# Making the third 512-row block of four rounds use seven products in its second layer, and planning with shorter tables

## The chip, the cores and the metric

The kernel runs on one core of a Trainium2 chip. The metric is the device time of one execution in microseconds (us); the median of three runs stands for a kernel. A profile of one further execution, taken by the hardware profiler, gives the start and length of every instruction on each engine: PE (TensorE matmuls; PEld its weight loads), DVE (VectorE), ACT (ScalarE), POOL (GpSimd) and SP (SyncE, which here only issues DMAs).

## What is computed

The input is x of shape (8, 2496, 256): eight batches of 2496 rows. The first half is a two-dimensional Fourier transform of every batch, of which the real part is kept:

```python
X = np.fft.fft(x, axis=1)
X = np.fft.fft(X, axis=2)
x = X.real.reshape(19968, 256)
```

The second half sends each of the 19968 rows to one of 8 experts, a network of two layers with 1024 hidden values, and weighs the result:

```python
logits = x @ w_gate
e = np.argmax(logits, axis=1)
h = np.maximum(x[rows of e] @ w1[e], 0.0)
y[rows of e] = h @ w2[e]
out = gate_w[:, None] * y
```

## The kernel before

**Two streams of work in one program.** The *mixing* of a batch (functions `first`, `second` and `route`, L325 to L460) computes the transform, the logits and the place of each row, and `send` (L462) scatters rows, 128 at a time, with an indirect DMA of POOL into a buffer `Xs` sorted by expert. The *experts* (`experts`, L728) take blocks of rows of one expert out of `Xs`, run both layers and scatter the result to the output, again with indirect DMAs of POOL (`put_row`, L235). Which block belongs to which expert is found on the chip by `plan` (L478), a chain of small DVE instructions on one partition. Its tables have `MOST` entries, 21, the largest number of blocks of any plan.

**Rounds.** `rounds()` (L130) fixes how many blocks are formed of each batch: small ones for batches 0 and 1, three blocks of 512 rows for batch 2, five blocks of 512 rows for each of the batches 3 to 6, and five of 512, seven of 256 and up to 21 of 128 for batch 7. While the blocks of batch b are worked on, the mixing of batch b+1 and the first 12 steps (`AHEAD`, L186) of that of batch b+2 are woven in. The main loop (L985 to L1018) lets `experts` run from `yield` to `yield` and, by a count of the work done, puts a step of mixing behind some of them; steps are given out over the first 60% (`SHARE`) of a round's second layers. In the first-layer part of a 512-row block only sends are put in. The order of all instructions on every engine is therefore written by this program; each engine works through its own list in that order.

**Blocks by seven products.** The first layer of every 512-row block of batches 3 to 7 is made with seven products of half size in place of eight (`seven`, L613; the choice is `halved`, L191). Its sums are made by DVE out of PSUM and written to `hT` (L634 to L653). The second layer of some blocks is made by seven products as well (`lower`, L659; the choice is `quartered`, L196): in batches 3 to 6 the blocks with index 3 and 4, in batch 7 all of its 512- and 256-row blocks. Otherwise the second layer is the plain one (L874 to L885): for each 128 rows eight matmuls into a PSUM tile `py`, one scaling by ACT (L881), one indirect DMA.

What `lower` needs beyond the plain form:

- sums of weights (`Below`, L593 to L606): four additions of 128x512 on POOL for a 512-row block. If the block before it is plain, they are issued between that block's four `py` parts (`soon`, L875); otherwise in the block's own first layer (`below.step()`, L814);
- sums of hidden values: four DVE instructions at L809 in the first layer, two at L860 (`s2`) and two at L864 (`s4`) in the second;
- five PSUM banks shared with the first layer (`pse`, one buffer each of a to e), and after the products six DVE additions on halves of `y` (L682, L700, L706, L712) and ACT scalings (L678, L687).

While a block's second layer runs, the next block's rows are turned (`turn`, L576): per 256 rows a DVE transpose (L582) and an ACT change of sign (L585), then four DVE additions (L570 to L573). The mixing steps put their own DVE instructions (the fold of `xq`, L295 to L306; L408 and L410 for the rows) and ACT copies (`t<-pr` L372, `zz` L379, `zs` L405) into the same lists, and share one pool of three PSUM buffers (`pm_`) for `pr`, `p`, `s` and `rk`.

Of the kernel before, what the change touches and what calls it, by code (L numbers as in the profile page):

```python
# [15 lines left out]
ALU = mybir.AluOpType  # L16
ACTF = mybir.ActivationFunctionType
AX_X = mybir.AxisListType.X
PSUM = bass.MemoryType.PSUM

B, S, D = 8, 2496, 256
# [14 lines left out]
E, F = 8, 1024  # L36
# [14 lines left out]
def bc(ap, axis, n):  # L51
    shape = list(ap.shape)
    shape.insert(axis, n)
    return ap[tuple([slice(None)] * axis + [None])].to_broadcast(shape)
# [75 lines left out]
def rounds():  # L130

    want = [((256, 2), (128, 4)), ((256, 4),)] + [((512, B),)] * (B - 2)
    plan, used = [], 0

    def full(done, size):
        return max(0, -(-(done - used - E * (size - 1)) // size))

    for b in range(B):  # L140
        done = (b + 1) * S
        now = []
        for size, most in want[b]:
            k = min(full(done, size), most)
            if k:
                now.append((size, k, False))
            used += size * k
        if b == B - 1:
            k = full(done, BLK)
            used += BLK * k  # L150
            now.append((BLK, k, False))
            now.append((REST, (NT - used + E * (REST - 1)) // REST, True))
        plan.append(now)
    return plan
# [33 lines left out]
MOST = max(k for now in rounds() for _, k, _ in now)  # L188


def halved(b, size):  # L191

    return size == 512 and b > 2 or size == 256 and b == B - 1


def quartered(b, size, at):  # L196

    return halved(b, size) and (b == B - 1 or at >= 3)


def block_consts():
# [14 lines left out]
def kernel(ctx: ExitStack, tc, x, w_gate, w1, w2, out):  # L216
    nc = tc.nc
    vec, act, pool = nc.vector, nc.scalar, nc.gpsimd
# [50 lines left out]
    con, k = {}, 0  # L269
# [205 lines left out]
    bk = {n: bt[:, lo:hi] for n, (lo, hi) in where.items()}  # L475
    gone = bk["cap"]

    def plan(b, size, k, last):  # L478

        nonlocal gone  # L480

        def one(name, *dims, dt=F32):
            return cp.tile([1, *dims], dt, tag="p_" + name, name="p_" + name, bufs=2 if name == "gone" else 1)

        nb, ni = one("nb", E), one("ni", E, dt=I32)
        ce, ex, rb, n = one("ce", E), one("ex", E), one("rb", E), one("n", E)
        lo = one("lo", E, E)
        vec.tensor_tensor(nb[:], base[0:1], gone[:], op=ALU.subtract)
        vec.tensor_scalar(ni[:], nb[:], size - 1.0 if last else 0.0, None, op0=ALU.add)
        vec.tensor_scalar(ni[:], ni[:], size.bit_length() - 1, None, op0=ALU.logical_shift_right)  # L490
        vec.tensor_copy(nb[:], ni[:])
        vec.tensor_tensor(lo[:], bk["low"].rearrange("p (a b) -> p a b", a=E), bc(nb[:], 1, E), op=ALU.mult)
        vec.reduce_sum(ce[:], lo[:], axis=AX_X)
        vec.tensor_tensor(ex[:], ce[:], nb[:], op=ALU.subtract)
        yield
        vec.scalar_tensor_tensor(rb[:], ex[:], -float(size), gone[:], op0=ALU.mult, op1=ALU.add)
        ge, ei = one("ge", MOST, E), one("ei", MOST)
        val, eq, rw = one("val", MOST, E + 1), one("eq", MOST, E + 1), one("rw", MOST)
        vec.tensor_tensor(ge[:], bc(bk["i"], 2, E), bc(ce[:], 1, MOST), op=ALU.is_ge)
        vec.reduce_sum(ei[:], ge[:], axis=AX_X)  # L500
        yield
        vec.tensor_tensor(eq[:], bc(ei[:], 2, E + 1), bc(bk["e9"], 1, MOST), op=ALU.is_equal)
        vec.memset(val[:, :, E:E + 1], float(E * CAP))
        vec.scalar_tensor_tensor(val[:, :, 0:E], bc(bk["i"], 2, E), float(size), bc(rb[:], 1, MOST),
                                 op0=ALU.mult, op1=ALU.add)
        yield
        vec.tensor_tensor(val[:], val[:], eq[:], op=ALU.mult)
        vec.reduce_sum(rw[:], val[:], axis=AX_X)
        tab = cp.tile([1, 2, MOST], I32, tag="p_tab", name="p_tab", bufs=4)
        vec.tensor_copy(tab[:, 0], rw[:])  # L510
        vec.tensor_scalar(tab[:, 1], ei[:], E - 1.0, None, op0=ALU.min)
        if last:
            cnt = cp.tile([1, 1], I32, name="cnt")
            vec.tensor_copy(cnt[:], ce[:, E - 1:E])
            tabs["cnt"] = cnt
        if not last:

            vec.tensor_scalar(n[:], ex[:], -1.0, float(k), op0=ALU.mult, op1=ALU.add)
            vec.scalar_tensor_tensor(n[:], n[:], 0.0, nb[:], op0=ALU.max, op1=ALU.min)
            nxt = one("gone", E)  # L520
            vec.scalar_tensor_tensor(nxt[:], n[:], float(size), gone[:], op0=ALU.mult, op1=ALU.add)
            gone = nxt
        yield
        tabs[b, size, last] = tab
# [203 lines left out]
    def experts(todo):  # L728
# [35 lines left out]
        for k, (b, size, last, at) in enumerate(todo):  # L764
# [24 lines left out]
            def step():  # L789
                if chores:  # L790
                    chores.popleft()()
                elif more:
                    more.step()

            both = quartered(b, size, at)
            below = None
            if both:
# [36 lines left out]
            if follow:  # L834
                while follow[:3] not in tabs:
                    yield 0, False
                fetch_some(k + 1, 2)
                while follow[0] not in whole:
                    yield 0, follow[0] < LATE
                fetch_some(k + 1, 2)  # L840
                turned = turn(*follow[:2], xbs[0][0])
                if halved(*follow[:2]):
                    left = more or Left(got[0][0])
                if not both and size == follow[1] == BIG and quartered(*follow[:2], follow[3]):
                    soon = Below(got[0][1], pool)
# [61 lines left out]
    def close(b):  # L907

        for size, k, last in rounds()[b]:
            yield from plan(b, size, k, last)  # L910
# [158 lines left out]
```

## Time and profile before

| | |
|---|---|
| median of three runs | 1270.7 us (1270.32 to 1275.03) |
| the profiled execution | 1270.37 us, of which the span from first to last instruction is 1268.5 us |
| busy in the span | PE 1212.5 us, PEld 1083.6, DVE 773.6, POOL 445.7, ACT 421.5 |
| granted TensorE clock | 0.980 of full speed on the mean, 1.00 from 300 us to 1240 us |
| second layer of the third block (index 2) | batch 3: 419.80 to 441.82 us, batch 4: 564.83 to 586.85, batch 5: 709.86 to 728.78, batch 6: 848.39 to 862.21 |

How to read the views: the page's first part gives busy time, share of the span and number of instructions for each engine. In a group or a timeline row, the line is that of kernel.py, then come engine, operation, output<-inputs and shapes; L221 is the helper that records every matmul, so matmuls are told apart by their output tile. In the timeline, the first number is the start in us from the beginning of the span, the second how long the merged row lasted; `x16` is the number of instructions merged, and a bracket says how long the engine had been idle before and what ended that. One fp32 matmul appears as two rows' worth of records, so that `x16` are eight matmuls.

### The profile page before, as it was taken

The page shows a single profiled execution, that of the slowest core. Times are in us where ns is not written, and L with a number is a line of the kernel's source. Part 1 is how long each engine was busy: PE and PEld are TensorE (multiplying, and loading weights), DVE is VectorE, ACT ScalarE, POOL GpSimd, SP SyncE. Part 2 cuts the span into 40 slices and gives each one's busy share as a digit, 9 for nine tenths or more (in the row PEclk, how much of TensorE's full clock was granted, in tenths as well). Part 3 has the DMA queues.
Part 4 walks back from the last instruction along what each step waited for, and adds up shares of the span by engine and source line. Part 5 has one row for each costly group of instructions (what it writes and reads, how often), then busy time and mean ns, then how long its engine had stood idle before and what let it go on. Part 6 is the DMA issues. An engine that isn't in the chain of part 4 may idle for free.

```text
span 1268.5 us, 22212 instructions
## 1 busy us (share of the span) xinstructions
PE 1212.5 (96%) x7289; PEld 1083.6 (85%) x7289; DVE 773.6 (61%) x1884; ACT 421.5 (33%) x1087; POOL 445.7 (35%) x527
## 2 busy tenths in 40 slices
PE   5759999999999999999999999999999999999996
PEld 4548987876788899888998999889999999999995
DVE  4546334443465788576866588686788884444662
ACT  1423332332243433434243433432332322222222
POOL 0145427145116522472226612561462331111112
PEclk9869999999999999999999999999999999999997
DMA  8769898765348454573336435443444348777786
GB/s 239 246 194 334 306 311 305 193 223 176 124 151 254 139 148 154 165 249 114 101 127 207 136 117 171 133 153 96 146 130 159 104 157 288 278 284 270 270 292 231
DMA packets 163216, 249.79 MB, mean 197 GB/s; under 512 B 118601, under 2 KB 130227, under 8 KB 143516
## 3 DMA queue, kind: packets, MB, share of 16 engines
q1 hardware_dynamic: 146327, 203.28, 49.9%
q0 software_dynamic: 15888, 42.14, 9.2%
q10 hardware_dynamic: 885, 2.94, 0.7%
q8 instruction: 59, 0.97, 0.3%
q14 instruction: 57, 0.47, 0.1%
HBM read 194.91 MB, written 54.83 MB: 197 GB/s over the span
## 4 chain that ended last, share of the span: by engine, by line
PE 71%; issue 16%; DMA 4%; POOL 4%; DVE 3%; ACT 0%; POOLq 0%; SPq 0%; DVEq 0%; ACTq 0%
PE py L221 19%; PE a L221 10%; PE c L221 10%; PE d L221 7%; PE ph L221 6%; PE p L221 6%; PE b L221 5%; PE e L221 3%; PE s L221 3%; POOL out_dram L236 3%; DMA xq<-in_x_dram 1%; POOL Xs L236 1%; DMA t<-Td 1%; DMA w<-c_w 1%; DMA Xs<-rows,pi 0%
## 5 line engine op out<-in xcount | busy, mean ns | idle before, releaser
L236 POOL DMA_INDIRECT out_dram<-y,ro x163 | 161.0, 988 | 633.8 <-ACT y L678 297.9
L221 PE MATMUL py<-w_sb,hT 128*128 128x256 f32 x1504 | 340.3, 380 | 0.0
L221 PEld LDWEIGHTS py<-w_sb,hT 128*128 128x128 f32 x1504 | 282.0, 191 | 36.1 <-issue 1.0
L236 POOL DMA_INDIRECT Xs<-rows,pi x160 | 163.7, 1023 | 113.7 <-DVE rows L410 55.0
L221 PE MATMUL ph<-xT,w_sb 128*128 128x128 f32 (+2 forms) x992 | 173.0, 331 | 9.8 <-DVE ro L782 8.7
L221 PEld LDWEIGHTS ph<-xT,w_sb 128*128 128x128 f32 x992 | 137.7, 194 | 34.2 <-issue 16.5
L221 PE MATMUL a<-xT,w_sb 128*128 128x256 f32 (+1 forms) x512 | 118.1, 358 | 0.3 <-DVE xT L582 0.2
L827 DVE TENSOR_SCALAR hT<-ph 128x512 f32<-128x512 f32 x43 | 29.7, 690 | 127.7 <-PE ph L221 68.9
L585 ACT ACTIVATE xT<-xT 128x256 f32<-128x256 f32 (+1 forms) x94 | 36.5, 388 | 185.8 <-DVE xT L582 135.7
L221 PEld LDWEIGHTS a<-xT,w_sb 128*128 128x128 f32 x512 | 88.6, 191 | 10.6 <-DVE xT L582 1.3
L881 ACT ACTIVATE y<-py,xb 128x256 f32<-128x256 f32 x97 | 45.8, 473 | 154.4 <-PE py L221 152.6
L634 DVE TENSOR_TENSOR hT<-hT,b 128x512 f32<-128x512 f32 x57 | 39.2, 688 | 80.6 <-PE b L221 53.9
L408 DVE COPY lg<-p 128x16 f32<-128x16 f32 x80 | 13.8, 172 | 113.8 <-ACT zs L405 113.7
L644 ACT ACTIVATE hT<-a 128x512 f32<-128x512 f32 x57 | 34.0, 597 | 140.2 <-PE a L221 140.2
L221 PE MATMUL s<-xq,w 104*112 104x256 f32 (+2 forms) x208 | 61.5, 420 | 11.6 <-DVE xq L297 8.9
L582 DVE STREAM_TRANSPOSE xT<-xb 128x512 f32<-128x512 f32 (+1 forms) x94 | 58.7, 627 | 12.7 <-DMA xb<-Xs 12.7
L469 POOL CAST pi<-due 128x1 int32<-128x1 f32 x140 | 42.2, 301 | 68.8 <-ACT due L468 68.7
L221 PE MATMUL a<-w_sb,hT 128*128 128x128 f32 x528 | 66.0, 276 | 0.0
L221 PE MATMUL p<-table,zz 128*128 128x145 f32 (+1 forms) x320 | 58.3, 308 | 8.0 <-DVE rows L410 6.6
L221 PE MATMUL d<-w_sb,hT 128*128 128x128 f32 x528 | 65.5, 275 | 0.0
L221 PEld LDWEIGHTS a<-w_sb,hT 128*128 128x128 f32 x528 | 63.2, 192 | 0.7
L221 PEld LDWEIGHTS d<-w_sb,hT 128*128 128x128 f32 x528 | 62.2, 192 | 0.0
(144 smaller groups left out, 2086.0 us busy)
## 6 DMA issues: line engine op xcount, KB each, us to landing
w_sb<-in_moe_w_dram SPq DMA_DIRECT2D x132, 1024.0 KB, 7.0
xq<-in_x_dram SPq DMA_DIRECT2D x24, 896.0 KB, 8.6
xb<-Xs SPq DMA_DIRECT2D x112, 128.0 KB, 3.3
Td<-t SPq DMA_DIRECT2D x18, 448.0 KB, 3.3
t<-Td SPq DMA_DIRECT2D x8, 768.0 KB, 9.5
t<-Td SPq DMA_DIRECT2D x8, 640.0 KB, 9.2
xb<-Xs SPq DMA_DIRECT2D x52, 64.0 KB, 5.9
xb<-Xs SPq DMA_DIRECT2D x100, 32.0 KB, 5.4
```

What stands on the lines that cost most here:

```text
L221: nc.tensor.matmul(o, lhsT=lhsT, rhs=rhs, start=start, stop=stop, **kw)
L236: return unordered(pool.indirect_dma_start(out=dst, out_offset=bass.IndirectOffsetOnAxis(ap=idx, axis=0), in_=rows, in_offset=None, bounds ...
L408: vec.tensor_copy(lg[:, k:k + 2], p3[:, NY:NY + 2 * E].rearrange("p (m e) -> p m e", m=2))
L469: pool.tensor_copy(idx, due[:])
L582: vec.transpose(free(xT[:], 256 * h, [32, n // 32], [BIG, 2], [1, 32]), free(xb, 512 * h, [64, n // 32], [1, 2], [2, 32]))
L585: act.activation(odd, odd, ACTF.Copy, scale=-1.0)
L634: vec.tensor_tensor(h12, h11, b[:], op=add)
L644: act.activation(h11, a[:], ACTF.Relu)
L827: vec.tensor_scalar(o, ph[:], 0.0, None, op0=ALU.max)
L881: act.activation(y[:, i % 2], py[:], ACTF.Copy, scale=meta[:, i, 1:2])
```

## The change

Index 2 is added to the blocks whose second layer is made by seven products, which concerns one block in each of the batches 3 to 6. In `plan`, the tables get as many entries as the plan has blocks (k) in place of 21.

```diff
 def quartered(b, size, at):
 
-    return halved(b, size) and (b == B - 1 or at >= 3)
+    return halved(b, size) and (b == B - 1 or at >= 2)
...
         vec.scalar_tensor_tensor(rb[:], ex[:], -float(size), gone[:], op0=ALU.mult, op1=ALU.add)
-        ge, ei = one("ge", MOST, E), one("ei", MOST)
-        val, eq, rw = one("val", MOST, E + 1), one("eq", MOST, E + 1), one("rw", MOST)
-        vec.tensor_tensor(ge[:], bc(bk["i"], 2, E), bc(ce[:], 1, MOST), op=ALU.is_ge)
-        vec.reduce_sum(ei[:], ge[:], axis=AX_X)
+        ge, val, eq = (one(name, MOST, E + 1)[:, 0:k] for name in ("ge", "val", "eq"))
+        ei, rw = (one(name, MOST)[:, 0:k] for name in ("ei", "rw"))
+        count = bk["i"][:, 0:k]
+        vec.tensor_tensor(ge[:, :, 0:E], bc(count, 2, E), bc(ce[:], 1, k), op=ALU.is_ge)
+        vec.reduce_sum(ei, ge[:, :, 0:E], axis=AX_X)
         yield
-        vec.tensor_tensor(eq[:], bc(ei[:], 2, E + 1), bc(bk["e9"], 1, MOST), op=ALU.is_equal)
+        vec.tensor_tensor(eq, bc(ei, 2, E + 1), bc(bk["e9"], 1, k), op=ALU.is_equal)
         vec.memset(val[:, :, E:E + 1], float(E * CAP))
-        vec.scalar_tensor_tensor(val[:, :, 0:E], bc(bk["i"], 2, E), float(size), bc(rb[:], 1, MOST),
+        vec.scalar_tensor_tensor(val[:, :, 0:E], bc(count, 2, E), float(size), bc(rb[:], 1, k),
                                  op0=ALU.mult, op1=ALU.add)
         yield
-        vec.tensor_tensor(val[:], val[:], eq[:], op=ALU.mult)
-        vec.reduce_sum(rw[:], val[:], axis=AX_X)
+        vec.tensor_tensor(val, val, eq, op=ALU.mult)
+        vec.reduce_sum(rw, val, axis=AX_X)
         tab = cp.tile([1, 2, MOST], I32, tag="p_tab", name="p_tab", bufs=4)
-        vec.tensor_copy(tab[:, 0], rw[:])
-        vec.tensor_scalar(tab[:, 1], ei[:], E - 1.0, None, op0=ALU.min)
+        vec.tensor_copy(tab[:, 0, 0:k], rw)
+        vec.tensor_scalar(tab[:, 1, 0:k], ei, E - 1.0, None, op0=ALU.min)
```

k is 2 and 4 (batch 0), 4 (batch 1), 3 (batch 2), 5 (batches 3 to 6), and 5, 7 and 21 (batch 7). Behind the changed lines, line numbers of the changed kernel are higher by one. As the program writes the lists out, the block with index 2 now gets its weight sums between the four `py` parts of the block with index 1, the block with index 3 gets its own in its first layer, and the mixing steps that lay between the `py` parts of block 2 lie between the products of `lower`. With those of `lower`'s yields, the number of yields of a second layer stays eight.

## Prediction

> **What bounds the kernel now.** I read three views: the page's first and fourth part, the timeline of the stretches that change, and the windows over the same stretches.
>
> ```profile
> PE 1212.5 (96%) x7289; PEld 1083.6 (85%) x7289; DVE 773.6 (61%) x1884; ACT 421.5 (33%) x1087; POOL 445.7 (35%) x527
> PE 71%; issue 16%; DMA 4%; POOL 4%; DVE 3%; ACT 0%; POOLq 0%; SPq 0%; DVEq 0%; ACTq 0%
> ```
>
> PE is busy 96% of the span, and the chain that ended last is mostly PE. So the time falls by what PE no longer does, and rises by every new wait of PE. The 96% say nothing of single stretches; those are in the windows (stretch, length, then busy time and count of PE, PEld, DVE, ACT, POOL, then clock, DMA share, GB/s):
>
> ```profile
> 564.83:586.85 22.02, 21.14 (x118) 18.88 (x116) 15.80 (x26) 8.72 (x24) 10.87 (x11) 1.00 0.17 57
> 709.86:728.78 18.92, 18.92 (x109) 17.29 (x108) 9.15 (x18) 7.83 (x22) 9.97 (x10) 1.00 0.14 54
> 848.39:862.20 13.81, 13.81 (x65) 12.19 (x64) 9.78 (x15) 3.60 (x8) 9.98 (x10) 1.00 0.16 55
> 624.47:636.98 12.51, 12.51 (x114) 12.51 (x113) 10.21 (x20) 2.34 (x6) 0.00 (x0) 1.00 0.08 30
> ```
>
> The first three are the plain second layer of block 2 in batches 4, 5 and 6; batch 3 (419.80 to 441.82) is as long as batch 4. The last is a block that already uses seven products. The lesson is in the third and fourth rows: 13.81 us is what 32 plain matmuls take without work of the mixing between them, 12.51 us what seven products take (7 x 1.79). **The most that a block can give is 1.30 us**, four blocks 5.2. In batch 4, DVE is busy 15.80 of 22.02 us; there it has little room.
>
> The timeline of PE shows what a wait behind another engine looks like: a `p` stands idle 0.77 us until ACT has made `t<-pr`, although ACT is nearly idle: its list holds a sign change (L585) ahead of it, and that waits for a DVE transpose.
>
> ```profile
> 573.11 0.48 PE L221 MATMUL p<-table,t 120*128 120x120 f32 x2 [0.77 <-ACT t L372]
> 586.85 1.03 PE L221 MATMUL a<-xT,w_sb 128*128 128x256 f32 x4
> 841.38 1.13 PE L221 MATMUL c<-xT,ws 128*128 128x256 f32 x4 [0.24 <-DVE hT L640]
> 123.13 2.00 PE L221 MATMUL ph<-xT,w_sb 128*128 128x256 f32 x8 [1.17 <-DVE hT L827]
> ```
>
> **The change part by part. What it adds per block.** On DVE four L809 (0.68 to 0.77 us where nothing disturbs them), two L860 and two L864 (0.69), six additions on y (0.38 to 0.42): 2.9 + 1.4 + 1.4 + 2.4 = 8.1 us. On POOL four additions at 1.28: 5.1 us. ACT keeps about its work: one copy and six scalings in place of four. No DMA is added; the scatters of y go out two and two. The issue list of SP keeps its order. The matmul of 128 columns is proven on this chip: 112 records in 12.51 us, 112 ns each, against 216 ns in the plain form. The Trainium skill ("TensorE: Matmul & The Clock Gate", section "Back-to-back issue gap") says that halved columns do not halve the time of a weight load with its matmul (about 81 ns for 128 columns, 131 for 512); read between them, an estimate from that page gives a ratio of 0.83, some 20 us a block, and the change would cost 25 us. The row of this case is for fp32 and decides.
>
> **Batches 3 and 4: the gain is taken back by the order of DVE's and ACT's lists.** In before, 22.02 us are 13.81 of `py`, 6.9 of side work (`pr`, eight `p`, two `s`) and 1.3 of idle (0.77 in the row above, the rest in gaps that only the distance of the starts shows). After: 12.5 + 6.9 + new idle. The first wait: the second matmul of the first `p` comes after products 0, 3, 1, `pr`, product 5 and one matmul, at 4 x 1.79 + 0.14 + 0.14 = 7.4 us. DVE must by then have done, counted from the stretch's start with the spacing of the rows at 624.47: the last L653 and two L809 to 2.4, two L860 to 3.6, the fold (L306 1.18, L295 and L296 0.67, L297 0.16, spaced closer) to 6.0, two L864 to 7.2, one addition of weights to 7.8, the transpose to 8.4; ACT's sign change and `t<-pr` follow to 8.9. Idle 1.4 (a little of the 1.5 is made up by the spacing). The second: the seventh `p`-group needs a `zz` which stands on ACT behind two scalings L678, and these behind DVE's additions L712 and L682 of product 4: 0.7. The third: the same chain once more, behind L410, 0.4. Sum 12.5 + 6.9 + 2.5 = 21.9: **-0.1 us each, -0.2 for both**. From both sides: all idle gone, -2.6 each (22.02 - 19.4); POOL's additions falling on the fold as in before (L295 and L297 there took 1.64 and 1.69 in place of 0.67 and 0.16, 2.5 more), +2.4 each. I take the middle sum, since POOL's additions now move out of this stretch to the one before.
>
> **Batch 5.** Before: 18.92 = 13.81 + 5.1, no idle. After: no fold, so the first `p` waits only to 8.1 (0.7); a `zz` behind the scalings of half 0 costs 1.2; and behind the last product no product stands any more between the side matmuls and the next block, so that `zz` waits there for L678 of half 1, thus for DVE's last L682: 0.9. 12.5 + 4.9 + 2.8 = 20.2: **+1.3**. Bounds: -1.3 (hidden) and +2.5 (each wait by as much as the largest, 1.2).
>
> **Batch 6.** No side work in block 2: 13.81 becomes 12.5, **-1.3**. But the additions of weights now lie in block 1, and there DVE is already late: PE's 0.24 at 841.38 is a wait for L640. What such an addition does to DVE, the timeline shows twice:
>
> ```profile
> 851.20 1.28 POOL L606 TENSOR_TENSOR ws<-w_sb 128x512 f32<-128x512 f32 x1
> 853.81 1.28 POOL L606 TENSOR_TENSOR ws<-w_sb,ws 128x512 f32<-128x512 f32 x1
> 851.14 1.38 DVE L510 CAST p_tab<-p_rw 1x21 int32<-1x21 f32 x1
> 853.31 2.07 DVE L570 TENSOR_TENSOR xs<-xT 128x256 f32<-128x256 f32 x1
> ```
>
> The cast lasts 0.17 elsewhere, L570 0.41: each began before or beside an addition and ended with it, 1.2 to 1.7 us late. The Trainium skill ("SBUF — State Buffer", section "Who interferes with whom") has it as a lock: a DVE instruction with two SBUF inputs, or a copy or cast in its fast mode, and a POOL instruction that reads SBUF shut each other out, while one with a PSUM input does not. The rows agree, and so do L634 and L653, which keep their 0.69; by the page up to 4 x 1.28 per block could fall on DVE. My sum: three of the four fall on DVE (3 x 1.2 = 3.6), the plans of batch 7 in that place get shorter by 0.8 and 0.7, leaving 2.05 of new idle at about 841: **+2.0 - 1.3 = +0.7**. Bounds: -1.6 (no hit; the 0.24 goes) and +3.5 (four hits, no shorter plans: 4 x 1.2 - 1.3).
>
> **Block 1 in batches 3 to 5.** The same additions fall there, but DVE has been done by 548.56 in batch 4, and PE needs a sum of DVE's again at 553.6, 0.9 into the first layer that begins at 552.74: 5 us of room against 3 x 1.2. I cost it at nothing; without the cover it is the third rival. Block 3's additions go to its own first layer, as block 4's do already.
>
> **Plans.** A plan has some eight instructions over 21 entries:
>
> ```profile
> L499 DVE TENSOR_TENSOR p_ge<-bt,p_ce 1x168 f32<-1x168 f32 x11 | 3.5, 315 | 0.0
> ```
>
> 168 elements take 315 ns, 64 take 207 to 219, 8 take 154; with k of 3 to 5 a plan saves 0.7 to 1.1 us. Eleven plans save about 10 us of DVE, nearly all beside PE. One is on the path: at 117.8 to 122.3 (batch 1), behind which L827 is late and PE stands 1.17 at 123.13. There it gives **-1.0**, and then the matmul before it on PE is what is late. The first plan, 63 to 80 us, lies behind POOL's scatters (1.27 each) and gives nothing. Bounds for all plans: 0 and -2.
>
> **Sum.** -0.2 + 1.3 + 0.7 - 1.0 = +0.8. The profiled execution took 1270.37 us (span 1268.5 and 1.87 around it), the median is 1270.7, so nothing has to be corrected: 1270.4 + 0.8 = **1271.2 us**.
>
> **The rivals.** *Only PE counts* (waits hidden elsewhere, as ACT and DVE catch up): 4 x -1.3 - 1.0 = -6.2, 1264.2; with before's own idle gone too, 1262.5. For it speaks that the blocks 3 and 4 in the same batches show 12.51 without idle; against it, that these have no side work between their products, which batches 3 to 5 have in block 2. *POOL holds DVE in block 1 of every batch:* if each addition costs 1.8 (the largest of the rows above), four cost 7.2, and against 5.1 us of room and 0.8 of shorter plans 1.3 is left in each of batches 3 to 5, and in batch 6 +4.3 in place of +0.7; it decides as soon as one addition costs over 1.5. Sum -0.2 + 1.3 + 3 x 1.3 + 4.3 - 1.0 = +8.3: 1278.7, slower. For it speaks the 2.07 of L570; against it that most hits were 1.2 and that PSUM inputs are not hit. *The change does nothing:* the instruction lists of the changed kernel have 28 more products, so it could only be the plans, 1269.4 to 1270.4; it lies within the forecast's range.
>
> **How the numbers follow.** Forecast 0.70, only PE counts 0.16, POOL holds DVE 0.14. The bounds of the forecast's parts do not all fall together; adding them as squares gives about -5 and +5: 1266 to 1276. With the edge of the first rival, 1265.0 to 1276.5. Half a per cent, 6.35 us, is about what a measurement of this kernel can tell from no change. Faster by more than that: half of the first rival, 0.08. Slower by more: most of the second, 0.12. Within: 0.80.
>
> **What would show it.** The second layer of block 2 should last 21.9 us (batches 3 and 4), 20.2 (batch 5), 12.5 (batch 6), with PE's idle bracketed by ACT t L372 at the first `p` and by ACT zz at later ones; the idle at the last `c<-xT,ws` ahead of batch 6's block 2 should be about 2.3; the 1.17 at 123 should be near 0.1. I am wrong if `p` shows no idle in batches 3 and 4 (first rival), or if first layers of block 2 stand in batches 3 to 5 (second).

## The result and the profile after

The changed kernel takes 1282.88 us (median of six runs), the kernel before, on the same chips, 1274.12: the ratio is 1.0065, 95% interval 1.0045 to 1.0085. **It is slower, by some 8.3 us by the ratio (8.8 between the medians).** The range on record ended at 1276.5. Of the 11.7 us by which the forecast of 1271.2 missed, 3.4 lie in the kernel before, whose median was 1270.7 when the forecast was made and is 1274.12 over the six runs here.

The profiled execution took 1281.78 us, with a span of 1279.7, 11.2 over before. First the page's first part:

```profile
PE 1211.8 (95%) x7481; PEld 1083.6 (85%) x7481; DVE 802.9 (63%) x1940; ACT 417.1 (33%) x1091; POOL 467.8 (37%) x543
```

PE is busy as long as before (1212.5): what the seven products save was eaten up somewhere. DVE has 29 us more. The page does not tell where the 11 us are. A table of stages does; each number is the distance from the start of one block's first layer to that of the next, read off PE's timeline:

| us | before | after | difference |
|---|---|---|---|
| block 1, batches 3 / 4 / 5 / 6 | 25.98 each | 26.39 / 26.31 / 26.31 / 26.31 | +0.4, 3 x +0.33 |
| block 2, batch 3 | 34.11 | 34.64 | +0.53 |
| block 2, batch 4 | 34.11 | 34.63 | +0.52 |
| block 2, batch 5 | 31.01 | 32.68 | +1.67 |
| block 2, batch 6 | 26.42 | 33.41 | **+6.99** |
| all other blocks of these rounds | | | 0 within 0.03 |

These add up to 11.1. Ahead of batch 3's blocks the changed kernel is 1.1 us earlier; from the start of batch 7's blocks to the end of the span it loses 1.2, of which 1.1 in one wait (PE behind DVE hT L641, at 1051.01).

Now the windows over the second layer of block 2 in batches 4, 5 and 6 (stretch, length, busy time and count of PE, PEld, DVE, ACT, POOL, clock, DMA share, GB/s), and over most of the first layer ahead of it in batch 6, in two parts:

```profile
565.00:587.53 22.53, 20.33 (x166) 19.16 (x164) 18.34 (x40) 8.13 (x25) 11.34 (x12) 1.00 0.14 51
710.88:731.46 20.58, 18.55 (x158) 17.91 (x157) 13.76 (x32) 7.04 (x23) 8.47 (x11) 1.00 0.17 57
859.71:872.21 12.50, 12.50 (x113) 12.50 (x112) 10.74 (x25) 2.34 (x6) 0.98 (x1) 1.00 0.03 9
```

```profile
838.80:849.70 10.90, 5.34 (x25) 4.37 (x23) 10.14 (x29) 1.85 (x6) 9.26 (x13) 0.97 0.86 253
849.70:856.25 6.55, 6.54 (x16) 5.26 (x17) 3.19 (x5) 2.09 (x6) 3.42 (x6) 0.54 0.40 148
```

The products do what they should: 12.50 us in batch 6. The loss lies ahead of them. In the first stretch PE works half of the time while DVE (10.14 of 10.90) and POOL (9.26) are nearly full; in the second PE is busy all the time, but the granted clock is 0.54. PE's timeline has the same two things, and the two larger waits of batch 4 and the largest of batch 5:

```profile
574.00 0.48 PE L221 MATMUL p<-table,t 120*128 120x120 f32 x2 [1.27 <-ACT t L372]
581.02 0.70 PE L221 MATMUL p<-table,t 120*128 120x120 f32 x4 [0.70 <-ACT zz L379]
726.09 0.77 PE L221 MATMUL p<-table,zz 128*128 128x145 f32 x4 [1.12 <-ACT zz L379]
849.71 2.08 PE L221 MATMUL c<-xT,ws 128*128 128x256 f32 x4 [5.56 <-DVE hT L641]
851.57 1.91 PE L221 MATMUL a<-xT,w_sb 128*128 128x256 f32 x4
853.28 1.91 PE L221 MATMUL b<-xs,ws 128*128 128x256 f32 x4
854.99 1.43 PE L221 MATMUL d<-xT,w_sb 128*128 128x256 f32 x4
856.25 1.03 PE L221 MATMUL c<-xs,ws 128*128 128x256 f32 x4
```

An idle of 5.56 us (0.24 before), and behind it four products that start 1.86, 1.71, 1.71 and 1.26 apart where 0.865 is usual: 3.1 us more. 5.3 + 3.1 - 1.3 (the products' gain) = 7.1, near the table's 6.99.

Why is DVE late? Its timeline and POOL's, from 826 to 845 in batch 6:

```profile
826.93 1.93 DVE L451 TENSOR_TENSOR pos<-pos,oh 128x80 f32<-128x80 f32 x1
830.88 1.92 DVE L494 TENSOR_TENSOR p_ex<-p_ce,p_nb 1x8 f32<-1x8 f32 x1
839.05 2.05 DVE L505 SCALAR_TENSOR_TENSOR p_val<-bt,p_rb 1x56 f32<-1x56 f32 x1
843.12 1.90 DVE L490 TENSOR_SCALAR p_ni<-p_ni 1x8 int32<-1x8 int32 x1
```

```profile
827.46 1.29 POOL L607 TENSOR_TENSOR ws<-w_sb 128x512 f32<-128x512 f32 x1
831.48 1.30 POOL L607 TENSOR_TENSOR ws<-w_sb,ws 128x512 f32<-128x512 f32 x1
839.73 1.28 POOL L607 TENSOR_TENSOR ws<-w_sb,ws 128x512 f32<-128x512 f32 x1
843.71 1.27 POOL L607 TENSOR_TENSOR w_sb<-w_sb 128x512 f32<-128x512 f32 x1
```

Each of the four additions on POOL has one small DVE instruction beside it that begins 0.5 to 0.7 us ahead of the addition's start and ends with it. Undisturbed these take 0.24, 0.15, 0.19 and 0.16 us; the next plan's L494, with no addition beside it, is one such row:

```profile
836.61 0.15 DVE L494 TENSOR_TENSOR p_ex<-p_ce,p_nb 1x8 f32<-1x8 f32 x1
```

So all four additions hit, that is, each holds a DVE instruction, and each costs DVE 1.7 to 1.9 us, together 7.1. DVE's first sum of block 2, here before and after, starts 3.28 us into the block before (which begins at 835.79) and 8.60 after (838.80):

```profile
839.07 0.67 DVE L634 TENSOR_TENSOR hT<-hT,b 128x512 f32<-128x512 f32 x1
```

```profile
847.40 0.67 DVE L635 TENSOR_TENSOR hT<-hT,b 128x512 f32<-128x512 f32 x1
```

That is 5.3 later: 7.1, less the 1.5 that the shorter plans save there and the 0.33 by which PE itself reaches the block later.

### The profile page after: what moved, and what is told of

Same layout as the page of the kernel before. It is cut to its first block, busy times and chain, and to the rows that moved or that the text cites. A ratio compares the mean times of both kernels' runs of the same rounds, so it can differ in the third digit from the quotient of the medians.

```text
span 1279.7 us, 22700 instructions
## 1 busy us (share of the span) xinstructions
PE 1211.8 (95%) x7481; PEld 1083.6 (85%) x7481; DVE 802.9 (63%) x1940; ACT 417.1 (33%) x1091; POOL 467.8 (37%) x543
## 5 line engine op out<-in xcount | busy, mean ns | idle before, releaser
L221 PE MATMUL py<-w_sb,hT 128*128 128x256 f32 x1248 | 283.0, 380 | 1.0 <-DVE hT L828 0.6
L221 PEld LDWEIGHTS py<-w_sb,hT 128*128 128x128 f32 x1248 | 233.1, 190 | 33.6 <-ACT y L882 1.9
L236 POOL DMA_INDIRECT Xs<-rows,pi x160 | 169.5, 1059 | 112.6 <-DVE rows L410 54.3
L221 PE MATMUL a<-w_sb,hT 128*128 128x128 f32 x656 | 81.6, 276 | 0.0
L221 PE MATMUL d<-w_sb,hT 128*128 128x128 f32 x656 | 81.1, 275 | 0.0
L221 PEld LDWEIGHTS a<-w_sb,hT 128*128 128x128 f32 x656 | 78.4, 192 | 0.9
L882 ACT ACTIVATE y<-py,xb 128x256 f32<-128x256 f32 x81 | 38.3, 473 | 121.9 <-PE py L221 111.8
L221 PEld LDWEIGHTS d<-w_sb,hT 128*128 128x128 f32 x656 | 77.1, 192 | 0.0
L221 PE MATMUL s<-xq,w 104*112 104x256 f32 (+2 forms) x208 | 61.5, 420 | 11.9 <-DVE xq L297 11.7
L221 PEld LDWEIGHTS p<-table,t 120*128 120x128 f32 x352 | 52.7, 203 | 16.2 <-issue 7.1
L221 PE MATMUL c<-xT,ws 128*128 128x256 f32 (+1 forms) x256 | 59.9, 361 | 6.7 <-DVE hT L641 6.7
```

What stands on the lines that cost most here:

```text
L221: nc.tensor.matmul(o, lhsT=lhsT, rhs=rhs, start=start, stop=stop, **kw)
L236: return unordered(pool.indirect_dma_start(out=dst, out_offset=bass.IndirectOffsetOnAxis(ap=idx, axis=0), in_=rows, in_offset=None, bounds ...
L882: act.activation(y[:, i % 2], py[:], ACTF.Copy, scale=meta[:, i, 1:2])
```

## The experiments

My theory: POOL's additions for block 2, moved into block 1, hold DVE there. Rivals: DVE has too much to do in any case (its additions for seven products), or the new plans cost the time. A second question was what makes PE wait in batches 3 to 5. The lengths of the stages in all kernels, as in the table above:

| us | block 1, b. 4 | block 2, b. 4 | block 2, b. 5 | block 2, b. 6 | ratio to before (interval) |
|---|---|---|---|---|---|
| before | 25.98 | 34.11 | 31.01 | 26.42 | |
| after | 26.31 | 34.63 | 32.68 | 33.41 | 1.0065 (1.0045 to 1.0085) |
| short plans alone | 25.99 | 34.10 | 31.01 | 25.90 | 0.9983 (0.9968 to 0.9997) |
| seven products, old plans | 26.86 | 34.80 | 32.85 | 34.28 | 1.0103 (1.0071 to 1.0135) |
| POOL's sums unused | 26.31 | 33.31 | 31.03 | 33.45 | 1.0033 (1.0019 to 1.0046) |
| POOL fills with zeros | 25.98 | 34.11 | 31.01 | 25.90 | one run, 1265.55 us |
| sums in own first layer | 25.98 | 34.62 | 32.66 | 24.59 | 0.9991 (0.9976 to 1.0006) |
| sums on DVE | 25.98 | 34.62 | 32.66 | 25.43 | 1.0000 (0.9985 to 1.0014) |
| batch 6 only | 25.98 | 34.10 | 31.01 | 24.60 | 0.9976 (0.9962 to 0.9990) |
| turning late | 25.98 | 35.73 | 35.12 | 24.59 | 1.0030 (1.0012 to 1.0047) |
| turning and scaling late | 25.98 | 32.63 | 31.28 | 24.59 | 0.9947 (0.9928 to 0.9966) |
| block 1, too | 26.65 | 34.89 | 32.31 | 24.59 | 1.0059 (1.0034 to 1.0084) |

**1. The halves of the change.** Short plans alone:

```diff
-    return halved(b, size) and (b == B - 1 or at >= 2)
+    return halved(b, size) and (b == B - 1 or at >= 3)
```

> The changed kernel with block 2 plain again: only the shorter plans are left. Theory (the loss of the change is POOL's four additions in block 1, which hold DVE): about 1.1 us faster than before through the idle PE time at 123 us, plus 0.2 for the 0.24 idle ahead of batch 6's block 2; ratio 0.999. Rival (something in the new plans, such as their place in DVE's list, costs the time): slower than before, by up to 8 us.

It was 2.2 us faster. In the stages, 0.5 of this lies in batch 6's block 2, where the 0.24 of idle and some wider spacing of the starts went. The other stages from batch 3 on are as long as before, so the rest lies ahead of them. The plans cost nothing. The other half, the kernel before with `at >= 2`:

> The other half of the change alone: seven products for block 2 with the additions on POOL in block 1, plans of 21 entries. Theory (in batch 6 DVE is late by the sum of what stands in its list): without the 0.8 and 0.7 us that the shorter plans save there, the idle of 5.6 us becomes about 7.0, PE's half clock stays about 3 us, and the 1.1 us at 120 us are lost again: about 2.5 us over the changed kernel, 11 over before. Rival (the plans' length is hidden behind POOL's additions): equal to the changed kernel but for the 1.1.

The idle in batch 6 was 6.74 us in place of 5.56, and block 1 lost 0.88 in place of 0.33: 1.010 as against 1.0065. The short plans do help in the place where DVE is late.

**2. POOL's additions without the products.** Block 2 is plain again, but the additions stay in block 1. They leave the weights alone:

```diff
+                idle = None
+                if not both and size == follow[1] == BIG and 2 < b < B - 1 and follow[3] == 2:
+                    idle = Below(got[0][1], pool)
+                    o, p, q = idle.due.pop()
+                    idle.due.append((idle.due[0][0], p, q))
...
+                if idle:
+                    idle.step()
```

> Block 2 is plain, the plans are short, but POOL makes the four additions for block 2 in block 1 all the same; nobody uses them (the fourth writes a scratch tile, so the weights stay as they are). Theory: the idle of 5.6 us ahead of the last product of the first half of batch 6's block 2 appears as in the changed kernel, with PE at half clock behind it (together about 8.4), and the plain second layer of block 1 is 0.33 us longer in each of batches 3 to 6: 8 to 10 us over the kernel with the short plans alone. Rival (the seven products themselves and DVE's own additions for them make DVE late): no such idle, within 1 us of the kernel with the short plans alone.

PE's timeline in batch 6:

```profile
840.88 2.08 PE L221 MATMUL c<-xT,ws 128*128 128x256 f32 x4 [5.39 <-DVE hT L641]
842.75 1.91 PE L221 MATMUL a<-xT,w_sb 128*128 128x256 f32 x4
```

The idle and the slow products are all there without one seven-product block: 33.45 against 25.90 us. This was the clearest of the tests. The total was 5.9 us over the short plans alone (7.4 by the stages), where I had expected 8 to 10, in part because batches 3 and 4 each became 0.8 us shorter: the additions for block 3, later on POOL than before, no longer fell on the fold ahead of `t<-pr`, and the 0.77 of idle behind that copy was gone.

**3. Is it what POOL reads?** In the same kernel `pool.memset(o, 0.0)` stands in place of each unused addition.

> As the kernel with the four unused additions on POOL in block 1, but POOL fills the scratch tiles with zeros in their place, which writes SBUF and reads nothing; second layers of block 2 plain. Theory (an addition on POOL holds DVE while it reads SBUF): DVE's small instructions in block 1 keep their 0.15 to 0.24 us, and the idle of 5.4 us in batch 6 does not come. Rival (any long POOL instruction, or POOL's writes, hold DVE): instructions of 1.9 us on DVE beside each fill, and an idle of several us.

No idle came (25.90). Beside one of the fills three instructions of the plan last some 0.3 us longer, beside the others none does. A fill is shorter than an addition, though:

```profile
829.78 0.56 POOL L881 MEMSET ws<- 128x512 f32 x1
```

So the fills are no full counter-test for the length; what is shown is that they do not hold DVE for their duration as additions do.

**4. The same additions elsewhere.** In the first layer of block 2 itself:

```diff
-                if not both and size == follow[1] == BIG and quartered(*follow[:2], follow[3]):
+                if not both and size == follow[1] == BIG and quartered(*follow[:2], follow[3]) and (b == B - 1 or follow[3] != 2):
```

> The changed kernel, but POOL makes the additions for block 2 in the first layer of block 2 itself, as for blocks 3 and 4. Theory: block 2 of batch 6 is back at 25.1 us from the start of its first layer to the next block (26.4 less 1.3), block 1 loses its 0.33; batches 3 to 5 keep their new waits (0.5, 0.5 and 1.7); in all about 0 to 1 us over before, 8.4 under the changed kernel. Rival (DVE has too much to do, wherever POOL adds): the idle moves to another product of block 2 and 5 us or more of the loss stay.

Batch 6 fell to 24.59 us, that is 26.42 less the idle of before, its wider spacing (0.5 together) and 1.3; block 1 was as before. The additions still ran beside DVE there. Sums that read PSUM kept their 0.69 us, as L641 does here beside the addition of 836.50 to 837.79; instructions that read SBUF alone could be held, as L810 beside the next addition, which takes 0.68 elsewhere:

```profile
836.89 0.69 DVE L641 TENSOR_TENSOR hT<-hT,c 128x512 f32<-128x512 f32 x1 [0.17 <-PE c L221]
840.09 1.45 DVE L810 SCALAR_TENSOR_TENSOR s<-hT 128x512 f32<-128x512 f32 x1
```

All holds of this first layer come to 1.1 us of DVE, and PE did not wait for them. And in block 1, but on DVE (`soon = Below(got[0][1], vec)`):

> The changed kernel, but DVE itself makes the additions for block 2, at the same places between the parts of block 1. Theory (an addition on POOL holds DVE for 1.7 to 1.8 us, one on DVE takes 0.68): DVE gets 4 x 1.1 = 4.4 us back, so the idle ahead of the last product in batch 6 falls from 5.6 to about 1.2 and the half clock behind it goes: about 7 us under the changed kernel. Rival (DVE is merely full and POOL's additions do not hold it): 2.7 us more work for DVE, so the idle grows to about 8 us.

```profile
839.27 1.13 PE L221 MATMUL c<-xT,ws 128*128 128x256 f32 x4 [0.57 <-DVE hT L641]
```

0.57 us of idle in place of 5.56, though DVE has four additions more. **An addition costs DVE 0.67 us when DVE makes it, and 1.7 to 1.9 when POOL makes it beside the plan in DVE's list.** The rival of a merely full DVE falls with these two.

**5. Where the gain is pure.** Seven products for block 2 in batch 6 alone, additions in its own first layer (`at >= (2 if b == B - 2 else 3)`):

> Seven products for block 2 in batch 6 alone, POOL's additions in that block's own first layer, short plans. Theory: 1.3 us (13.81 less 12.50) under the kernel with the short plans alone, that is about 3.5 us under before; the stretch of block 2 in batch 6 is 24.59. Rival (the 112 records of 128 columns bring nothing): equal to the kernel with the short plans.

The stretch shows the 1.3 us (24.60 against 25.90). The total, 3.0 us under before, cannot tell that from the short plans alone: the intervals overlap.

**6. What makes PE wait in batches 3 to 5.** On top of the kernel with the sums in the own layer, in block 2 of these batches only (`late`), the turning goes one product later:

```diff
         s4()
         step()
-        turn_some()
+        if not late:
+            turn_some()
         yield
         product(5, c)
...
         vec.tensor_tensor(high, u3, c[:], op=add)
+        if late:
+            turn_some()
         plus(u3, b)
```

> The kernel with POOL's additions in block 2's own first layer, and in block 2 of batches 3 to 5 the turning of the next block's rows is put one product later (first transpose and sign change behind product 5 in place of product 1). Theory (PE's first wait is ACT's copy t<-pr, which stands behind a sign change that waits for DVE's transpose): the idle of 1.27, 1.27 and 0.45 us ahead of the first p goes, the later ones (0.70 and 0.24; 1.12 and 0.36) stay: about 3 us under the kernel with the additions in the own layer. Rival (DVE is what is late, whatever the order): the idle stays or moves to a later p, no gain.

It failed: 5 us slower than the kernel it was made from, of which block 2 of batches 3, 4 and 5 shows 3.2 (-0.34, +1.11 and +2.46). The first wait did go, but the second grew; batch 4:

```profile
576.61 0.95 PE L221 MATMUL p<-table,t 120*128 120x120 f32 x4 [1.86 <-ACT zz L379]
577.35 1.25 PE L221 MATMUL p<-table,zz 128*128 128x145 f32 x4
578.39 2.88 PE L221 MATMUL d<-w_sb,hT 128*128 128x128 f32 x16
```

ACT's list and DVE's, of the same kernel, say why:

```profile
575.40 0.91 ACT L679 ACTIVATE y<-y,xb 128x256 f32<-128x256 f32 x2 [2.33 <-DVE y L683]
576.22 0.34 ACT L379 COPY zz<-p 128x240 f32<-128x240 f32 x1
```

```profile
573.30 0.42 DVE L571 TENSOR_TENSOR xs<-xT 128x256 f32<-128x256 f32 x1
573.82 0.42 DVE L572 TENSOR_TENSOR xs<-xT,xs 128x256 f32<-128x256 f32 x1
574.28 0.42 DVE L573 TENSOR_TENSOR xs<-xT,xs 128x256 f32<-128x256 f32 x1
574.62 0.42 DVE L574 TENSOR_TENSOR xT<-xT 128x256 f32<-128x256 f32 x1
574.96 0.41 DVE L683 TENSOR_TENSOR y<-y,b 128x256 f32<-128x256 f32 x1
```

My edit put the four additions of the turning ahead of L683; the scaling waits for L683, `zz` stands behind the scaling, and PE behind `zz`. With the scalings and the sends put behind the mixing steps as well:

```diff
         plus(u2, c)
-        scaled(0, 0, D)
-        send_rows(0)
+        if not late:
+            scaled(0, 0, D)
+            send_rows(0)
         step()
         yield
+        if late:
+            scaled(0, 0, D)
+            send_rows(0)
```

and the same for the second half behind the last yield.

> As with the turning later, and in the same blocks the scalings of y by ACT and their sends are put behind the mixing steps of that place instead of ahead of them. Theory (the copies zz stand behind scalings which wait for DVE's additions): the idle of 0.70 (batches 3 and 4), 1.12 and 0.36 (batch 5) goes, too; block 2 from first layer to next block 32.5 us in batches 3 and 4 and 31.0 or less in batch 5; with the first waits about 5 to 6 us under the kernel with the additions in the own layer, some 6 us under before. Rival: idle of the same size at other places, no gain.

**1261.22 us, 0.9947 of before: faster than both kernels.** What is left of the waits in batch 4:

```profile
572.94 0.77 PE L221 MATMUL p<-table,zz 128*128 128x145 f32 x4 [0.24 <-ACT t L321]
578.17 0.37 PE L221 MATMUL pr<-t,table 120*120 120x5 f32 x2 [0.24 <-ACT t L321]
```

Block 2 is now 1.5 us shorter than before in batches 3 and 4, 1.8 in batch 6; in batch 5 it is still 0.3 longer. The scalings late without the turning late were not run.

**7. One block more.** Block 1 of batches 3 to 5 as well, `at >= (1 if b < B - 2 else 2)`, additions in its own layer:

> The kernel with turning and scalings late, and block 1 of batches 3 to 5 uses seven products as well, its weight sums made by POOL in its own first layer. Theory (a block without side matmuls gives 1.3 us if DVE's list has room): block 1 falls from 25.98 to 24.7 in each of the three batches, 3.9 us in all, about 10 us under before. Rival (the plan in block 1's list, some 7 us of small DVE instructions, makes DVE late beside its 8 us of sums): PE idles 1 to 3 us in each of these blocks, and nothing is gained.

The rival was right about the waits. In batch 3, product 4 (the sixth in order) writes bank `c` a second time, and waits for the DVE sum that reads the bank, which stands behind the plan:

```profile
410.92 3.52 PE L221 MATMUL c<-ws,s 128*128 128x128 f32 x16 [3.27 <-DVE y L702]
```

The idle was 3.27, 1.67 and 2.02 us in the three batches; the kernel is slower than before (1.0059). The plan is not all of it: in batch 3, three of POOL's additions also held DVE instructions of block 1's own first layer, by 4.5 us together, and block 1 lasted 30.41 us there. And block 2 lasted 2.3 us longer in batches 3 and 4 than with both edits alone, and 1.0 in batch 5, with new waits of PE for POOL's own sums (0.72 and 0.84 in batches 4 and 5); why was not examined.

## Why the prediction was wrong

**The step that failed is "Batch 6".** It put the new idle at 2.05 (2.3 with the 0.24 of before) and the sum at +0.7, with +3.5 as the upper bound; measured were an idle of 5.56 and +6.99. The mechanism, POOL's additions holding DVE in block 1, was named; two terms of its price were off.

- *The price and the number of hits.* I took three hits at 1.2 us. There were four, at 1.69, 1.77, 1.86 and 1.74. The row that I had shown beside the cast, L570 at 2.07 for 0.41, already said 1.66; I chose the lowest of the rows for the middle value. Nor were "most hits" 1.2: of the 13 DVE instructions held beside block 2's additions in batches 3 to 6 of the kernel before, two lost 1.2 us, four 0.85 to 0.96 and seven 1.48 to 1.79. Even as a bound 4 x 1.2 was too low, though the second rival was priced with 1.8. That price stands in none of the rows shown beside it (1.66 is their largest); a cast in the same stretch of the kernel before has it, beside the third addition (0.16 elsewhere):

```profile
856.63 1.95 DVE L782 CAST ro<-xb 128x4 int32<-128x4 f32 x1
```

- *What PE loses behind an idle.* I priced only the wait. PE worked for another 6.5 us at a granted clock of 0.54, 3.1 us more; the clock was 0.50 from 848.96 to 855.79. No term stood for that. The Trainium skill ("TensorE: Matmul & The Clock Gate", section "What's actually happening") says that an idle window of about 3.4 us halves the clock until a window of work has passed; the idle of 5.56 and the 6.83 us at 0.50 agree with such a halving.

The second rival had the mechanism and the sign, and its sum, 1278.7 (+8.3), lies near the measured +8.3 and the +11.4 of the profile, but partly by luck: it put 3.9 us into the first layers of block 2 in batches 3 to 5, none of which waited, and +4.3 into batch 6, where it was +6.99. DVE's 5 us of room covered the hits, as the forecast said ("I cost it at nothing"). Neither of the two signs of being wrong that I had named came: `p` was idle in batches 3 and 4, and no first layer of block 2 stood in batches 3 to 5. What showed it was the idle in batch 6, of which I had given the size and no limit.

The other steps:

- *Batches 3 and 4*: -0.1 each; +0.53 and +0.52 measured. The first two waits are those named (1.27 and 0.70 against 1.4 and 0.7); the third, 0.24 against 0.4, is not: there `pr` waits for ACT's copy `t` of L321, and not a `p` for a `zz`. The second layer took 22.53 in place of 21.9. With the sum's 12.5 and 6.9 this leaves 3.1 for the waits: 2.2 in brackets, the rest only in the distance of the starts around them.
- *Batch 5*: +1.3; measured +1.67, with the waits 0.45, 1.12 and 0.36 against 0.7, 1.2 and 0.9. The sum took the side work as 4.9, where its own row gives 5.1; with 5.1, the 20.58 measured leave 3.0 for the waits, against 2.8, and again brackets show only 1.9 of it.
- *The products*: 12.50 us in batch 6, as the rows said.
- *Block 1*: 0; measured +0.33 to +0.4 in batches 3 to 6. DVE's second transpose was held up by two additions, ACT's sign change waited for it, the scaling L882 stood behind that, and a `py` weight load for its bank. I had looked for DVE's own cover and not for ACT's:

```profile
549.34 3.32 PEld L221 LDWEIGHTS py<-w_sb,hT 128*128 128x128 f32 x16 [0.47 <-ACT y L882]
```

- *Plans*: -1.0 at 123 us. In the profile after, PE's wait there was 1.45 and not 0.1, and the 512-row blocks still began 1.1 us earlier. The start of batch 3's blocks lies between 340.9 and 350.9 us over all profiles, so a single profile cannot tell it; the kernel with the short plans alone is 2.2 us faster (0.4 to 4.1 by the interval), which contains it.

The 1.1 us at 1051 in batch 7 stays open: the kernels with the old plans and with block 1 had it (1.11 each), others not; with the short plans alone there was 0.78 at another place, and with seven products in batch 6 alone the last 512-row block of batch 7 was 1.17 longer. I made no experiment on it.

## What to carry to other kernels

Before work is moved to a free engine, look at what runs beside it: an addition on POOL took 1.28 us there and 1.7 to 1.9 away from DVE, against 0.67 if DVE had made it; in this kernel it belongs where DVE reads PSUM or has room. An idle of PE of some us is to be priced with the slow clock behind it. And where engines work through written lists, each wait has a list behind it: one edit of the order moved the wait, and two together took most of it away.

## What was not expected of the hardware

- A DVE instruction on one partition with 8 elements is held as long as a large one: L494, 0.15 us, lasted 1.92. One of the four was a TENSOR_SCALAR on int32 with a single tensor input.
- The hold is longer than the addition: DVE's instruction began up to 0.68 us ahead of POOL's recorded start and still ended only with it, at most 0.11 us later. The Trainium skill ("SBUF — State Buffer", section "Who interferes with whom") gives the shared ports to whichever issues first; by these starts DVE was first and lost, unless POOL's recorded start is late.
- The clock fell after idles shorter than the 3.4 us named above, too: after 1.86 us in batch 4 of the kernel with late turning (0.50 from 576.92 to 580.33), and not after 1.85 us in batch 3 of the same execution. Block 2 took 35.73 us in batch 4 and 34.27 in batch 3, 1.45 less. What decided between the two is not shown. The windows around the end of each idle and behind it:

```profile
431.00:437.90 6.90, 6.25 (x46) 5.76 (x47) 3.88 (x14) 4.39 (x15) 3.77 (x4) 1.00 0.14 57
576.00:584.57 8.57, 7.73 (x47) 7.38 (x47) 4.17 (x14) 4.58 (x15) 3.79 (x4) 0.80 0.11 46
```
